# In three opening slots of an attention and gated-MLP kernel, VectorE's weight passes move behind the second maxima, and GpSimd's q/k split behind its weight split

## The chip, the core and the metric

The kernel runs on one core of a Trainium2 chip. A core has TensorE (PE, matrix products and transposes), VectorE (DVE), ScalarE (ACT), GpSimd (POOL) and SyncE (SP), which here only issues transfers. Each engine works through its own list of instructions in order and waits on semaphores for the others. The metric is the device time of one execution in microseconds, 771.0 us as the median of three runs of the kernel before.

## The reference

For 8 batches with 8 heads, 576 positions and 64 values per head:

```python
scores = (1.0 / np.sqrt(D)) * np.matmul(q, k.transpose(0, 1, 3, 2))
scores = np.where(block_i >= block_j, scores, -1000000000.0)   # blocks of 64 positions
attn = np.exp(scores - np.max(scores, axis=-1, keepdims=True))
attn = attn / (np.sum(attn, axis=-1, keepdims=True) + 1e-09)
x = np.matmul(attn, v)                      # then (8, 576, 512)
...
h = gelu_tanh(x @ w_in)                     # w_in 512 x 1024
u, v = h[..., :512], h[..., 512:]
v_n = (v - mu) / np.sqrt(var + 1e-06) * g_ln
v_s = np.einsum('ts,bsd->btd', w_sg, v_n) + b_sg[None, :, None]
out = x + (u * v_s) @ w_out
```

Everything is float32. Some of the weights arrive as 64-bit words (float64).

## The kernel before

The work is cut into 32 slots, one for a pair of heads (8 batches of 4 pairs). In a slot the kernel finishes the attention of pair n and begins the scores of pair n+1. To keep float32 accuracy on fast products, an operand is split into a high part (`qh`, `kh`, `wi_h`, `xh`) and the remainder (`ql`, `kl`, `wi_l`, `xl`), and three products high-high, low-high, high-low are summed.

For one pair (two heads, a = 0, 1), rows come in five groups i = 0 to 4 of growing width. `Scores.products` (L327) lets PE write scores to PSUM (`s`). `Scores.maximum` (L349) is DVE's: it copies the scores with the mask to `prob` and leaves the negated row maximum in `negm`. `Scores.exponent` (L364) is ACT's exponential of `prob` with that `negm`. The groups 4, 1 and 0 form the list `FIRST` (L388): eight maxima of up to 288 columns, here called the first maxima. `Scores.second` (L394) does groups 3 and 2: products, then four maxima of 448, 448, 320 and 320 columns (the second maxima), then four exponentials. `Values.turn` (L415) transposes `prob` on PE into `pA`, `pB`, `pC` and copies these to SBUF (`ptA`, `ptB`, `ptC`, half of them by DVE); `pB` and `pC` need the second exponentials. `Values.products` and `normalise` (L458, L477) multiply with v and scale (`ob`, `x`), and `split` (L485) makes `xh` and `xl`. `split_qk` (L112) splits the q and k of the pair after next on GpSimd: `qh`, `ql`, `kh`, `kl`, each for 576 columns; the next slot's scores read them.

While the first four slots run, the 64-bit weights are also converted. `load_weight` (L212) yields three times per group of parts (a part is 128 x 256): after the load and an ACTIVATE of ScalarE, after `Double.single` (L201), which on DVE is one TENSOR_SCALAR and two SCALAR_TENSOR_TENSOR for each part (the "passes over the weights", tile `w`), and after `split_weight` (L184), on GpSimd a CAST to `wi_h` and a subtraction to `wi_l`. Each call of `weight_half` runs one such third. The groups of the first four slots have 3, 2, 2 and 1 parts.

These four slots are written by `opening_slot` (L721). In them a switch (`written`) holds DVE, ACT and GpSimd to the order in which the code is written (PE always is); SP's transfers are placed by the scheduler. From the fifth slot on only PE's order is fixed, a scheduler places the rest, and the feed-forward products of a finished batch fill PE between the attention steps. The first of these are at the end of the fourth slot (`v_part`, tiles `accv`), which needs the converted weights of the v half.

Of the kernel before, what the change touches and what calls it, by code (L numbers as in the profile page):

```python
# [20 lines left out]
def kernel(  # L21
# [70 lines left out]
    def copy(e, dst, src):  # L92
        f = {"v": vector.tensor_copy, "a": scalar.copy, "g": gpsimd.tensor_copy}[e]
        return f(dst, src)
# [9 lines left out]
    def load_qk(n):  # L104
        b, h = PAIRS[n]
        q_f = sp.tile([P, S], F32, tag="q_f", name="q_f", bufs=1)
        k_f = sp.tile([P, S], F32, tag="k_f", name="k_f", bufs=1)
        nc.sync.dma_start(q_f, qT[b, h : h + 2].rearrange("a d s -> (a d) s"))
        nc.sync.dma_start(k_f, kT[b, h : h + 2].rearrange("a d s -> (a d) s"))
        raw[n] = (q_f, k_f)  # L110

    def split_qk(n):  # L112
        out = []
        for x, t in zip(raw.pop(n), "qk"):
            hi = sp.tile([P, S], F32R, tag=t + "h", name=t + "h", bufs=1)
            lo = sp.tile([P, S], F32R, tag=t + "l", name=t + "l", bufs=1)
            if n == 0:
                copy("v" if t == "q" else "a", hi, x)
                vector.tensor_tensor(lo, x, hi.bitcast(F32), op=ALU.subtract)
            else:  # L120
                copy("g", hi, x)
                behind["G"] = gpsimd.tensor_tensor(lo, x, hi.bitcast(F32), op=ALU.subtract)
            out += [hi, lo]
        qk[n] = out

    def load_v(n):
        b, h = PAIRS[n]
        v_f = v_bufs[n % 2]
        cols = slice(h * D, (h + 2) * D)
        nc.sync.dma_start(  # L130
            v_f[:, : NT - 1, :],
            v[b, : (NT - 1) * P, cols].rearrange("(j p) d -> p j d", p=P),
        )
        nc.sync.dma_start(v_f[:TAIL, NT - 1, :], v[b, S - TAIL :, cols])
        vals[n] = v_f
# [156 lines left out]
    def weight_half():  # L292

        while weights:
            said = next(weights[0][1], None)
            if said is not None:
                return said
            weights.popleft()
# [416 lines left out]
    def split_pending():  # L715

        for f in pending:
            f()
        pending.clear()

    def opening_slot(n, va):  # L721

        va.turn(0, "A")
        va.turn(1, "A")
        va.turn(0, "B")
        va.turn(1, "B")
        va.inverse()
        split_pending()
        va.turn(0, "C")
        va.turn(1, "C")  # L730
        load_v(n + 1)
        load_qk(n + 2)
        nx = Scores(n + 1)
        for p in nx.FIRST:
            nx.products(*p)
        va.turn_sums()
        weight_half()
        for p in nx.FIRST:
            nx.softmax(*p)
        weight_half()  # L740
        if n < Q - 1:
            nx.second()
            split_qk(n + 2)
            weight_half()
            va.products()
            va.normalise()
            pending.append(va.split)
        else:
            weight_half()
            va.products()  # L750
            va.normalise()
            va.split()
            nx.second()
        nv = Values(n + 1, nx)
        if n == Q - 1:
            nv.inverse()
            split_qk(n + 2)
        return nx, nv
# [118 lines left out]
```

## Time and profile before

| what | before |
|---|---|
| median of the runs shown | 771.0 us (768.85, 771.0, 771.5) |
| the profiled execution | 770.48 us, its span 768.7 us |
| busy share of the span | PE 98%, DVE 63%, ACT 57%, POOL 39% |
| first maximum of pairs 1, 2, 3, 4 | 15.68, 31.70, 45.79, 59.73 us |

The span runs from the first to the last instruction; the execution's own time is 1.8 us longer. A row of the timeline gives start, duration, engine, the line of the code (L60 for nearly all, a helper that records every operation), the operation, `out<-in` with sizes, and in brackets the idle time ahead of it with the engine that ended it. PEld is PE's loading of its stationary operand, which overlaps with the products. A busy share over the whole span hides that the opening slots have other limits than the rest, so the prediction looks at these by themselves.

### The profile page before, as it was taken

To read this page: it belongs to the slowest core of one execution; us is meant where nothing else is said; L and a number is where in the kernel's file an instruction comes from. 1 tells how busy PE (TensorE), PEld (TensorE's weight loads), DVE (VectorE), ACT (ScalarE), POOL (GpSimd) and SP (SyncE) were. 2 spreads that over 40 slices of the span, in tenths; PEclk is the share of its full clock that TensorE was granted. 3 is DMA by queue.
4 is the path that set the end of the run, shared out by engine and by line. 5 is a ranking of instruction groups with operands and counts; after the bars stand their busy time and mean duration, and the time that the engine had idled before them with its cause. 6 is when DMAs were issued, how large, how long until landed. Compare 5 with 4: busy or idle time off the path is not lost.

```text
span 768.7 us, 18262 instructions
## 1 busy us (share of the span) xinstructions
PE 751.7 (98%) x7106; PEld 711.2 (93%) x7106; DVE 483.5 (63%) x1477; ACT 438.3 (57%) x1096; POOL 299.2 (39%) x382
## 2 busy tenths in 40 slices
PE   8779998999999999999999999999999999999998
PEld 8778997989999899999999899998999989998998
DVE  6898789775945468544776348663495644942632
ACT  6666868558734767337754377544874467731600
POOL 3666695544234333243434234341234522322121
PEclk9989999999999999999999999999999999999999
DMA  8235233224232213312242112511124211120032
GB/s 261 82 103 178 64 107 92 77 90 133 85 119 62 63 64 109 94 47 63 64 140 78 33 61 76 172 48 48 49 91 141 63 42 53 53 88 17 1 124 93
DMA packets 46922, 65.84 MB, mean 86 GB/s; under 512 B 4082, under 2 KB 22514, under 8 KB 46836
## 3 DMA queue, kind: packets, MB, share of 16 engines
q1 hardware_dynamic: 46836, 64.67, 27.0%
q8 instruction: 56, 0.92, 0.5%
q14 instruction: 30, 0.25, 0.1%
HBM read 45.78 MB, written 18.87 MB: 84 GB/s over the span
## 4 chain that ended last, share of the span: by engine, by line
PE 92%; DVE 6%; ACT 1%; issue 1%; DMA 0%; POOL 0%; SPq 0%; DVEq 0%; ACTq 0%; POOLq 0%
PE accs L60 15%; PE accv L60 14%; PE acco L60 13%; PE accu L60 12%; PE s L60 10%; PE ob L60 10%; PE pB L60 5%; PE pC L60 5%; PE pA L60 3%; PE pd L60 2%; DVE w L60 2%; DVE prob L60 2%; PE pe L60 1%; ACT prob L60 1%; DVE vv L566 1%
## 5 line engine op out<-in xcount | busy, mean ns | idle before, releaser
L60 ACT ACTIVATE prob<-prob,negm 128x576 f32<-128x576 f32 (+3 forms) x320 | 176.4, 553 | 72.2 <-DVE negm L60 69.4
L60 DVE CUSTOM_DVE_ANT_0 prob<-s,mask 128x288 f32<-128x288 f32 (+3 forms) x320 | 121.5, 424 | 47.7 <-PE s L60 47.0
L60 POOL TENSOR_TENSOR xh<-x,xh 128x64 fp32r<-128x64 f32 x32 | 10.4, 325 | 205.5 <-DVE xh L60 145.4
L60 POOL TENSOR_TENSOR gl<-u,gh 128x288 fp32r<-128x288 f32 x64 | 51.8, 813 | 95.7 <-DVE gh L60 95.5
L60 PE MATMUL accu<-xh,wi_h 128*128 128x288 f32 x256 | 78.4, 306 | 0.0
L60 PE MATMUL accs<-ws_h,vh 128*128 128x288 f32 x256 | 77.9, 304 | 0.0
L60 PE MATMUL acco<-gh,wo_h 128*128 128x288 f32 x256 | 77.6, 303 | 0.0
L60 PE MATMUL accs<-ws_h,vl 128*128 128x288 f32 x256 | 75.6, 295 | 1.3 <-DVE vl L60 1.3
L60 PE MATMUL acco<-gl,wo_h 128*128 128x288 f32 x256 | 75.5, 295 | 0.0
L60 PE MATMUL accu<-xl,wi_h 128*128 128x288 f32 x256 | 75.5, 295 | 0.0
L60 PE MATMUL accs<-ws_l,vh 128*128 128x288 f32 x256 | 75.5, 295 | 0.0
L60 PE MATMUL accu<-xh,wi_l 128*128 128x288 f32 x256 | 75.4, 295 | 0.0
L60 PE MATMUL acco<-gh,wo_l 128*128 128x288 f32 x256 | 75.3, 294 | 0.0
L60 PE MATMUL accv<-wi_h,xh 128*128 128x512 f32 x160 | 65.3, 408 | 0.0
L60 DVE TENSOR_TENSOR u<-accs,u 128x288 f32<-128x288 f32 x64 | 29.1, 455 | 54.4 <-PE accs L60 53.9
L60 PE MATMUL accv<-wi_l,xh 128*128 128x512 f32 x160 | 63.0, 393 | 0.0
L60 PE MATMUL s<-kh,qh 64*128 64x288 f32 (+4 forms) x384 | 62.6, 322 | 0.0
L60 ACT ACTIVATION_READ_ACCUMULATOR prob<-prob,negm 128x1 f32 x320 | 59.9, 187 | 0.0
L60 PE MATMUL s<-kh,ql 64*128 64x288 f32 (+4 forms) x384 | 58.4, 301 | 0.0
L60 PE MATMUL s<-kl,qh 64*128 64x288 f32 (+4 forms) x384 | 57.3, 299 | 0.0
L60 ACT COPY vv<-accv 128x512 f32<-128x512 f32 x32 | 18.6, 581 | 67.1 <-PE accv L60 67.1
L60 PE MATMUL pB<-ident,prob 128*128 128x128 f32 x320 | 43.6, 283 | 8.5 <-DVE negm L60 6.8
(113 smaller groups left out, 2108.5 us busy)
## 6 DMA issues: line engine op xcount, KB each, us to landing
q_f<-in_qT SPq DMA_DIRECT2D x32, 288.0 KB, 3.6
k_f<-in_kT SPq DMA_DIRECT2D x32, 288.0 KB, 2.8
spill<-x SPq DMA_DIRECT2D x32, 288.0 KB, 2.9
xr<-spill SPq DMA_DIRECT2D x32, 288.0 KB, 2.9
out_T<-xr SPq DMA_DIRECT2D x32, 288.0 KB, 2.1
v_f<-in_v SPq DMA_DIRECT2D x32, 256.0 KB, 3.2
w<-in_w_in SPq DMA_DIRECT2D x16, 256.0 KB, 4.8
xr<-in_w_out SPq DMA_DIRECT2D x8, 256.0 KB, 2.7
```

What stands on the lines that cost most here:

```text
L60: return lambda *a, **k: pin(method(*a, **k), self.letter)
L566: tc.keep_in_program_order(nc.vector.scalar_tensor_tensor(x, x, stats[:rows, st, 0:1], g_bc[:rows, :], op0=ALU.subtract, op1=ALU.mult))
```

## The change

In the first three slots (n = 0, 1, 2) the second scores, maxima and exponentials are written ahead of DVE's passes over the weights, and GpSimd's weight split ahead of `split_qk`. The fourth slot keeps its order.

```diff
         weight_half()
         for p in nx.FIRST:
             nx.softmax(*p)
-        weight_half()
         if n < Q - 1:
             nx.second()
+            weight_half()
+            weight_half()
             split_qk(n + 2)
-            weight_half()
             va.products()
             va.normalise()
             pending.append(va.split)
         else:
+            weight_half()
             weight_half()
             va.products()
             va.normalise()
```

On DVE, in the second slot (the first maxima, of groups 4, 1 and 0, end above these rows; `prob0_3` is head 0, group 3; the ISA rows of `negm` alone read out the maximum that the row before them found). A piece of the difference:

```order
 L60 ISA prob1_0_115,negm_523<-s_539,mask_94 64x64
 L60 ISA negm_523 64x1
+L60 ISA prob0_3_111,negm_522<-s_586,mask_94 128x448
+L60 ISA negm_522 128x1
+L60 ISA prob1_3_121,negm_523<-s_587,mask_94 128x448
+L60 ISA negm_523 128x1
+L60 ISA prob0_2_109,negm_522<-s_598,mask_94 128x320
+L60 ISA negm_522 128x1
+L60 ISA prob1_2_119,negm_523<-s_599,mask_94 128x320
+L60 ISA negm_523 128x1
 L60 TENSOR_SCALAR w_566<-w_349 128x256
 L60 SCALAR_TENSOR_TENSOR w_566<-w_349,w_566 128x256
```

The four second maxima, which stood behind the slot's last pass over `w` and just ahead of `x`, now follow the first maxima at once.

On GpSimd, in the same slot (`q_f`, `k_f` are the loaded q and k; `w_566` and `w_570` the slot's two weight parts):

```order
-L60 CAST qh_616<-q_f_516 128x576
-L60 TENSOR_TENSOR ql_617<-q_f_516,qh_616 128x576
-L60 CAST kh_620<-k_f_517 128x576
-L60 TENSOR_TENSOR kl_621<-k_f_517,kh_620 128x576
 L60 CAST wi_h_125<-w_566 128x256
 L60 TENSOR_TENSOR wi_l_126<-w_566,wi_h_125 128x256
 L60 CAST wi_h_125<-w_570 128x256
 L60 TENSOR_TENSOR wi_l_126<-w_570,wi_h_125 128x256
+L60 CAST qh_620<-q_f_516 128x576
+L60 TENSOR_TENSOR ql_621<-q_f_516,qh_620 128x576
+L60 CAST kh_624<-k_f_517 128x576
+L60 TENSOR_TENSOR kl_625<-k_f_517,kh_624 128x576
```

The four instructions of the q/k split moved behind the four of the weight split; the buffers' numbers differ because they are now made later.

On SP the load of the next q, which waits for GpSimd to be done with the present one, moved behind the next v load and the store of `x` (`spill`), here in the first slot:

```order
+L130 DMA v_f0_101<-in_v 128x4x128
+L483 DMA spill_456<-x_453 128x576
 L108 DMA q_f_516<-in_qT 128x576
-L130 DMA v_f0_101<-in_v 128x4x128
-L483 DMA spill_456<-x_453 128x576
 L109 DMA k_f_517<-in_kT 128x576
```

The k load keeps its place. PE's and ScalarE's instructions stand in the same order as before.

## The prediction

> **What bounds the kernel now.** I read the busy shares and the chain of waits first, then the stretch that the change touches.
>
> ```profile
> PE 751.7 (98%) x7106; PEld 711.2 (93%) x7106; DVE 483.5 (63%) x1477; ACT 438.3 (57%) x1096; POOL 299.2 (39%) x382
> PE 92%; DVE 6%; ACT 1%; issue 1%; DMA 0%; POOL 0%; SPq 0%; DVEq 0%; ACTq 0%; POOLq 0%
> ```
>
> TensorE (PE) carries the chain nearly everywhere; VectorE (DVE) holds 6% of it. Part of those 6% lies in the three opening slots, where no feed-forward products exist yet. I measure a slot from the first maximum of one pair (`prob<-s,mask 128x288`) to the first maximum of the next: from 15.68, 31.70 and 45.79 us, the last ending at 59.73. The windows view gives their lengths and busy times (columns: length, then PE, PEld, DVE, ACT and POOL (GpSimd), granted clock, DMA):
>
> ```profile
> 15.68:31.70 16.02, 12.02 (x135) 10.63 (x135) 13.92 (x41) 10.01 (x30) 9.84 (x13) 0.89 0.47 142
> 31.70:45.79 14.09, 11.96 (x135) 10.86 (x135) 12.66 (x39) 9.28 (x28) 8.20 (x10) 0.88 0.29 92
> 45.79:59.73 13.94, 11.82 (x135) 10.72 (x135) 12.66 (x38) 9.17 (x28) 8.24 (x12) 0.88 0.34 98
> 59.73:100.00 40.27, 40.27 (x405) 36.45 (x405) 33.02 (x106) 31.52 (x83) 27.47 (x41) 1.00 0.37 117
> ```
>
> In the slots PE idles 2 to 4 us each while DVE is busy for nine tenths. From 59.73 on PE has no idle time, so whatever moves that instant moves the end by as much. I therefore price one number: the sum of three slot lengths, 44.05 us. Waits within them:
>
> ```profile
> PE pB L60 <- DVE negm L60: 6.8, 3, 3.5
> DVE prob L60 <- PE s L60: 2.6, 3, 1.2
> DVE ptB L60 <- PE pB L60: 0.6, 2, 0.4
> ```
>
> PE waits 6.8 us for the second maxima; DVE itself waits only 3.2 us for PE. So DVE's own row of work sets the slot. Here it is in the third slot, with the undisturbed weight part of the fourth slot (62.22) and the last part of the first slot (23.40) under it:
>
> ```profile
> 45.79 0.46 DVE L60 CUSTOM_DVE_ANT_0 prob<-s,mask 128x288 f32<-128x288 f32 x1 [0.88 <-PE s L60]
> 48.27 0.28 DVE L60 TENSOR_SCALAR w<-w 128x256 uint32<-128x256 uint32 x1
> 49.73 1.51 DVE L60 TENSOR_SCALAR w<-w 128x256 uint32<-128x256 uint32 x1
> 51.28 2.31 DVE L60 SCALAR_TENSOR_TENSOR w<-w 128x256 uint32<-128x256 uint32 x2
> 53.51 0.61 DVE L60 CUSTOM_DVE_ANT_0 prob<-s,mask 128x448 f32<-128x448 f32 x1
> 55.42 0.68 DVE L60 TENSOR_TENSOR x<-ob,rb 128x512 f32<-128x512 f32 x1
> 59.73 0.46 DVE L60 CUSTOM_DVE_ANT_0 prob<-s,mask 128x288 f32<-128x288 f32 x1 [0.60 <-PE s L60]
> ...
> 62.22 0.28 DVE L60 TENSOR_SCALAR w<-w 128x256 uint32<-128x256 uint32 x1
> 62.54 0.95 DVE L60 SCALAR_TENSOR_TENSOR w<-w 128x256 uint32<-128x256 uint32 x2
> ...
> 23.40 0.48 DVE L60 TENSOR_SCALAR w<-w 128x256 uint32<-128x256 uint32 x1
> 25.27 0.61 DVE L60 CUSTOM_DVE_ANT_0 prob<-s,mask 128x448 f32<-128x448 f32 x1
> ```
>
> A weight part is one TENSOR_SCALAR and two SCALAR_TENSOR_TENSOR. Alone it takes 1.27 us (62.22 to 63.49). In the third slot two parts take 5.24 us (48.27 to 53.51), because GpSimd splits q and k at that moment: the same TENSOR_SCALAR needs 0.28 us at 48.27 and 1.51 us at 49.73, ending just after GpSimd's 1.48-us subtraction. The two engines take turns.
>
> ```profile
> 48.69 0.84 POOL L60 CAST qh<-q_f 128x576 fp32r<-128x576 f32 x1 [2.57 <-PE s L60]
> 49.61 1.48 POOL L60 TENSOR_TENSOR ql<-q_f,qh 128x576 fp32r<-128x576 f32 x1
> 51.84 1.46 POOL L60 TENSOR_TENSOR kl<-k_f,kh 128x576 fp32r<-128x576 f32 x1
> ...
> 40.51 0.40 POOL L60 CAST wi_h<-w 128x256 fp32r<-128x256 f32 x1
> 40.99 0.73 POOL L60 TENSOR_TENSOR wi_l<-w,wi_h 128x256 fp32r<-128x256 f32 x1
> ...
> 67.19 0.66 POOL L60 CAST qh<-q_f 128x576 fp32r<-128x576 f32 x1
> 67.93 1.44 POOL L60 TENSOR_TENSOR ql<-q_f,qh 128x576 fp32r<-128x576 f32 x1
> 69.31 0.74 POOL L60 CAST kh<-k_f 128x576 fp32r<-128x576 f32 x1
> ```
>
> **The change, part by part.** Instructions stay the same in kind and number; PE's and ScalarE's orders are untouched, and so is everything from the fourth slot on.
>
> (1) The second maxima no longer stand behind the weight parts. ScalarE's second exponentials can follow its first ones, so PE's 6.8 us of waiting for `negm` goes. On DVE alone this only reorders work. (2) GpSimd's q/k split no longer runs beside the weight parts, so these lose most of the turn-taking. Both gain for DVE. (3) The price: GpSimd now splits q and k *behind* the weights, whose split waits for DVE's last part. The next slot's first scores read that qh, kh and kl. Before, the split ended at 53.30 (51.84 + 1.46), 6.4 us ahead of the next first maximum, and cost the path nothing; that cover is now gone. So the stall moves from "PE waits for negm" to "PE waits for kl", and the new slot is a sum along DVE, GpSimd and PE:
>
> a. eight first maxima: 45.79 to 48.27, 2.48.
> b. four second maxima: 53.51 to 55.42, 1.91.
> c. the first weight part, GpSimd still: 1.27, less some 0.07 by which such rows overlap, 1.2.
> d. the second part while GpSimd splits the first. Never seen alone; between 1.27 (no turn-taking) and 1.87 (23.40 to 25.27, the one part that ran beside a weight split). There its TENSOR_SCALAR waited too (0.48 against 0.28); now GpSimd can only start after it, so I take 1.87 - 0.20 = 1.67.
> e. GpSimd's split of that last part: 0.40 and 0.73 with their gap, 40.51 to 41.72, plus 0.07 of release: 1.28.
> f. the q/k split: undisturbed 4.3 (67.19 to the end of kh at 70.05, where kl could start, plus 1.44), in the old place 4.61 (48.69 to 53.30). DVE's cast of xh now meets it once, at about the price that CAST qh shows, 0.84 - 0.66 = 0.18. I take 4.5.
> g. from kl to the first maximum: PE's remaining products and the release, 0.70, from this row to 45.79, 0.64, plus 0.06:
>
> ```profile
> 45.15 0.29 PE L60 MATMUL s<-kl,qh 64*128 64x288 f32 x2
> 47.78 0.36 PE L60 MATMUL s<-kl,qh 64*128 64x448 f32 x2
> 56.95 1.85 PE L60 MATMUL pC<-ident,prob 128*128 128x128 f32 x10
> 13.48 1.25 PE L60 MATMUL pC<-ident,prob 128*128 128x128 f32 x10
> ```
>
> Sum 13.74, against 14.09 and 13.94: -0.35 and -0.20. The first slot has three parts, 13.74 + 1.67 = 15.41 against 16.02: -0.61. Together **-1.2 us**. With d and f at their low ends the loops are 13.14 and 14.41, together -3.4; with c, d and f at their high ends 14.12 and 15.99, together +0.2.
>
> What runs beside it costs nothing: DVE's x, ptA, ptB, xh and ptC take at most 3.7 us after d (from 55.42 to 59.13, where the wait of 0.60 before 59.73 begins; a wait for pB is in it), while e and f take 5.8. The q load now goes out after the spill and when the later ql is done, about 11 us into a slot; the next CAST qh stands 8.5 us into the following one, 11 us later, and the load takes 3.6. GpSimd's xh and xl follow kl, run beside DVE's maxima (0.61 us at 53.51, though GpSimd was at its weight split from 53.30 on) and are done before the next weight part.
>
> ```profile
> q_f<-in_qT SPq DMA_DIRECT2D x32, 288.0 KB, 3.6
> ```
>
> **The clock is the second term.** A windows view cut into stretches of 3.41 us shows the granted clock (the column after the POOL entry):
>
> ```profile
> 20.61:24.02 3.41, 1.80 (x28) 1.50 (x24) 2.82 (x5) 1.29 (x6) 3.25 (x5) 1.00 0.59 169
> 37.67:41.09 3.42, 1.29 (x11) 0.87 (x9) 3.32 (x9) 1.01 (x3) 3.18 (x6) 1.00 0.51 164
> 41.09:44.50 3.41, 3.41 (x18) 3.41 (x18) 3.15 (x10) 2.86 (x9) 0.74 (x2) 0.50 0.42 130
> 51.33:54.74 3.41, 1.53 (x15) 1.03 (x11) 3.31 (x7) 0.97 (x5) 3.25 (x5) 1.00 0.46 106
> 54.74:58.15 3.41, 3.17 (x15) 3.18 (x16) 3.00 (x11) 2.88 (x10) 0.97 (x2) 0.50 0.48 167
> ```
>
> After a stretch with PE busy 1.29 or 1.53 us the clock is halved for one stretch; after 1.80 it isn't. Today the half clock falls on the transposes (pC takes 1.85 instead of 1.25) and costs what DVE waits for PE: the 3.2 us above. These are inside the old slot lengths and leave with them. In the new slot the second exponentials end at 2.41 us (54.16 to 56.57) after the first ones, which are over at 51.72 (54.16 less the wait of 2.44), 5.93 us into the slot:
>
> ```profile
> 54.16 0.67 ACT L60 ACTIVATE prob<-prob,negm 128x448 f32<-128x448 f32 x1 [2.44 <-DVE negm L60]
> 56.57 0.56 ACT L60 COPY ptA<-pA 128x512 f32<-128x512 f32 x1
> ```
>
> So pC ends about 8.9 us in; then PE idles until kh (8.54 + 2.9 = 11.4) and, after 0.5 us of products, until kl (13.0). Some 3.6 idle us of 4.1 stand together, and the halved stretch now falls behind them, on the scores. PE's last product for the first of the second maxima ends at 48.14, 2.35 us into the slot, and DVE wants it at 2.48: only 0.13 us of slack. A halved stretch costs PE up to 1.7 us (half of 3.41), a lucky one falls on later products and costs 0. The middle, 0.85, in two of the three slots, is **+1.7 us**; bounds 0 and 5.1.
>
> [...]
>
> **Sum.** -1.2 + 1.7 = +0.5 us on the profiled execution, which took 770.48 with a span of 768.7. That gives 771.0, which is also the median of the runs shown (768.85 to 771.5). Forecast: no change that can be told; a measurement of this kernel tells about 0.3%, 2.3 us.
>
> **Rivals.**
> *The clock stays full* (chance 0.22). The gap is cut by the scores that need only kh, and 1.80 busy us kept the clock up. Then -1.2 stands alone: 769.3, and 767.1 at the low ends of d and f. About a third of this case is below the 0.3% bound.
> *GpSimd doesn't gate* (0.03). If the q/k split were hidden, DVE's row would bound: 2.48 + 1.91 + 1.2 + 1.67 + 3.34 (x to ptC without the wait) + 0.95 for the scores = 11.6, 2.4 less per slot: -7, 763.5. Against it: the split would have to end by 10.6, but starts at 8.5 and takes at least 4.3.
> *Slower: the half clock lands on the scores in every slot* (0.15). Then DVE's second maxima, now with 0.13 us of cover instead of 5.2 us of weight parts, wait 1.7 each time: -1.2 + 5.1 = +3.9, 774.4; 775.8 with the high ends. It decides from 3.5 us of clock loss on, two full hits.
> That the order isn't changed as said is ruled out by the rows of the new order.
>
> **Chances.** Forecast 0.60, the three rivals 0.22, 0.03 and 0.15. Faster: 0.08 + 0.03 + 0.01 = 0.12; slower 0.15; same 0.73. The range 768.8 to 773.3 takes in the open clock with middle prices and one full hit more than forecast, and leaves out the outer ends of the rivals, 2 in 10.
>
> **What would show it.** Right: DVE's slots of about 15.4, 13.7 and 13.7 plus clock losses; weight parts after the second maxima in 2.9 us a pair instead of 5.2; "PE pB waits for negm" gone and "PE s waits for POOL kh or kl" in its place, 2 to 4 us a slot; POOL in the chain where DVE's w stood; the 0.50 stretches just after a kl. Wrong: slots near 11.6 (GpSimd hidden), weight parts still at 2.6 us each (turn-taking stays), or a first maximum that doesn't follow kl by 0.7 us.

## The result, and the profile after

| what | before | after |
|---|---|---|
| median of five executions each | 770.13 us (768.66 to 771.5) | 775.68 us (773.3 to 776.41) |
| ratio, with its 95% interval | | 1.0069 [1.0045, 1.0092] |
| the profiled execution | 770.48 us, span 768.7 | 773.3 us, span 771.5 |
| first maximum of pairs 1, 2, 3, 4 | 15.68, 31.70, 45.79, 59.73 us | 15.47, 31.32, 47.04, 62.57 us |
| sum of the three slots | 44.05 us | 47.10 us |

The kernel became 0.7% slower, about 5.5 us. The page's busy shares and its chain of waits, of the kernel after:

```profile
PE 752.5 (98%) x7106; PEld 711.2 (92%) x7106; DVE 480.2 (62%) x1477; ACT 437.9 (57%) x1096; POOL 298.8 (39%) x382
PE 89%; DVE 3%; POOL 2%; ACT 2%; DMA 2%; issue 1%; SPq 0%; POOLq 0%; ACTq 0%
```

GpSimd (POOL) is in the chain now, and DVE's share fell from 6% to 3%. In the slots the chain reaches DVE's last weight pass over ScalarE's exponentials (ACT, 2%) and not over DVE's maxima. That this link costs time isn't shown: the part's two SCALAR_TENSOR_TENSOR take 1.38 us here (39.11) and 1.38 us in the second slot of a kernel below, the second half of the change alone (33.17), whose chain has no such link there. DVE is busy 3.3 us less (480.2 against 483.5). The slots, and with them the fourth, in the windows view of the kernel after (length, then PE, PEld, DVE, ACT and POOL busy, granted clock, DMA):

```profile
15.47:31.32 15.85, 11.01 (x133) 9.67 (x133) 12.71 (x41) 9.81 (x30) 9.02 (x12) 0.95 0.39 124
31.32:47.04 15.72, 12.63 (x133) 11.23 (x133) 11.34 (x39) 9.06 (x28) 7.85 (x12) 0.83 0.28 90
47.04:62.57 15.53, 13.21 (x135) 11.82 (x135) 11.56 (x38) 9.22 (x28) 8.07 (x12) 0.79 0.25 78
62.57:81.48 18.91, 18.91 (x178) 16.51 (x178) 15.45 (x48) 12.84 (x36) 12.97 (x21) 1.00 0.59 176
```

DVE has 1.1 to 1.3 us less to do in each slot (11.34 against 12.66 in the second), yet the second and third slots are 1.6 us longer, at a granted clock of 0.83 and 0.79 where before it was 0.88. The fourth slot is as long as before (18.91 us, there 59.73 to 78.64). The waits of these slots in the kernel after (in all, times, longest):

```profile
POOL wi_h L60 <- DVE w L60: 22.8, 7, 7.4
DVE prob L60 <- PE s L60: 10.5, 6, 2.7
PE s L60 <- POOL kh L60: 7.2, 3, 3.8
PE s L60 <- POOL kl L60: 2.9, 3, 1.1
```

PE's wait for `negm` is gone. PE now waits 10.1 us for kh and kl, 3.4 a slot, and DVE waits 10.5 us for PE. GpSimd idles some 7 us at the start of each slot, until the first weight part is done, and is the one waited for at its end. The second slot on DVE, after:

```profile
31.32 0.46 DVE L60 CUSTOM_DVE_ANT_0 prob<-s,mask 128x288 f32<-128x288 f32 x1 [2.69 <-PE s L60]
...
33.81 0.07 DVE L60 DVE_READ_ACCUMULATOR2_ANT negm<- 64x1 f32 x1
35.68 0.62 DVE L60 CUSTOM_DVE_ANT_0 prob<-s,mask 128x448 f32<-128x448 f32 x1 [1.80 <-PE s L60]
...
37.60 0.29 DVE L60 TENSOR_SCALAR w<-w 128x256 uint32<-128x256 uint32 x1
...
38.79 0.29 DVE L60 TENSOR_SCALAR w<-w 128x256 uint32<-128x256 uint32 x1
...
40.41 0.68 DVE L60 TENSOR_TENSOR x<-ob,rb 128x512 f32<-128x512 f32 x1
...
42.66 1.51 DVE L60 CAST xh<-x 128x576 fp32r<-128x576 f32 x1
47.04 0.46 DVE L60 CUSTOM_DVE_ANT_0 prob<-s,mask 128x288 f32<-128x288 f32 x1 [2.27 <-PE s L60]
```

The two weight parts take 2.81 us (37.60 to 40.41), where they took 5.24. But ahead of the second maxima, at 35.68, DVE stands idle for 1.80 us. PE shows why. Its timeline has the first scores for the second slot above, then a piece of that slot's second scores, and at the foot the first scores for the third slot:

```profile
28.61 0.40 PE L60 MATMUL s<-kh,qh 64*128 64x288 f32 x2 [3.81 <-POOL kh L60]
30.10 0.61 PE L60 MATMUL s<-kl,qh 64*128 64x288 f32 x2 [0.95 <-POOL kl L60]
...
35.07 0.57 PE L60 MATMUL s<-kl,qh 64*128 64x448 f32 x2
...
44.75 0.40 PE L60 MATMUL s<-kh,qh 64*128 64x288 f32 x2 [2.14 <-POOL kh L60]
46.23 0.40 PE L60 MATMUL s<-kl,qh 64*128 64x288 f32 x2 [0.95 <-POOL kl L60]
```

The last product for the first of the second maxima ends at 35.64 (35.07 + 0.57), 4.3 us into the slot; before it was 2.35. Between 30.10 and 35.64 PE waits for nobody, but these two products take 0.57 us where the same two took 0.36 before (47.78). The windows of 3.41 us show the reason, the granted clock (after POOL):

```profile
26.25:29.67 3.42, 0.53 (x4) 0.30 (x4) 2.35 (x5) 1.21 (x2) 3.27 (x3) 1.00 0.39 114
29.67:33.08 3.41, 2.98 (x23) 2.92 (x24) 1.76 (x9) 0.00 (x0) 2.06 (x4) 0.50 0.60 189
33.08:36.49 3.41, 3.41 (x20) 2.61 (x20) 1.61 (x11) 2.60 (x9) 0.00 (x0) 0.50 0.01 2
43.32:46.73 3.41, 1.03 (x12) 0.80 (x14) 1.45 (x2) 0.72 (x2) 3.33 (x5) 1.00 0.30 87
46.73:50.15 3.42, 3.42 (x25) 3.02 (x25) 2.56 (x16) 0.54 (x2) 1.14 (x2) 0.50 0.27 86
50.15:53.56 3.41, 3.41 (x26) 2.94 (x28) 2.16 (x9) 3.41 (x12) 0.00 (x0) 0.50 0.00 0
```

After a stretch in which PE is busy 0.53 or 1.03 us, the clock is halved for two stretches, 6.83 us, not for one. They begin among the first scores and cover the second scores too. Such a run of halved stretches is called a closing below.

### The profile page after: what moved, and what is told of

The parts are those of the page before. It is cut to its first block, busy times and chain, and to the rows that moved or that the text cites. A ratio compares the mean times of both kernels' runs of the same rounds, so it can differ in the third digit from the quotient of the medians.

```text
span 771.5 us, 18262 instructions
## 1 busy us (share of the span) xinstructions
PE 752.5 (98%) x7106; PEld 711.2 (92%) x7106; DVE 480.2 (62%) x1477; ACT 437.9 (57%) x1096; POOL 298.8 (39%) x382
## 4 chain that ended last, share of the span: by engine, by line
PE 89%; DVE 3%; POOL 2%; ACT 2%; DMA 2%; issue 1%; SPq 0%; POOLq 0%; ACTq 0%
PE accs L60 15%; PE accv L60 14%; PE acco L60 13%; PE accu L60 12%; PE s L60 10%; PE ob L60 10%; PE pC L60 4%; PE pB L60 4%; PE pA L60 3%; PE pd L60 2%; ACT prob L60 2%; PE pe L60 1%; DMA k_f<-in_kT 1%; POOL kl L60 1%; DVE vv L566 1%
## 5 line engine op out<-in xcount | busy, mean ns | idle before, releaser
L60 POOL TENSOR_TENSOR xh<-x,xh 128x64 fp32r<-128x64 f32 x32 | 10.5, 328 | 197.0 <-DVE xh L60 136.9
L60 PE MATMUL s<-kl,qh 64*128 64x288 f32 (+4 forms) x384 | 59.4, 309 | 3.0 <-POOL kl L60 2.9
L60 PEld LDWEIGHTS s<-kh,qh 64*128 64x128 f32 x384 | 37.4, 191 | 17.5 <-POOL kh L60 7.9
```

What stands on the lines that cost most here:

```text
L60: return lambda *a, **k: pin(method(*a, **k), self.letter)
```

## The experiments

My theory after the result: the sum of the steps without the clock holds (15.41 + 13.74 + 13.74 = 42.89 us for the three slots), and the rest, 47.10 - 42.89 = 4.2 us, is the clock, halved because PE idles while GpSimd splits q and k. The first rival: the sum itself is too small, and the wait for GpSimd costs what the clock seems to. The second: one of the two halves of the change does the harm. The kernel before was run beside each; its median was 770.44 us in both groups of timed runs.

**Keep PE busy in the gap.** The kernel after with 20 transposes of the identity, whose result nobody reads, in the gap after `pC`. They take 0.12 us each at full clock (20 in 2.40 us, at 25.32 below).

```diff
         nx = Scores(n + 1)
+        if n:
+            warm(bank("warm"), 20)
         for p in nx.FIRST:
             nx.products(*p)
```

> The changed kernel, and in slots 2 to 4 twenty more transposes of the identity on PE, into a PSUM bank that nobody reads, between the transposes of pC and the next scores, where PE idles 3.8, 2.1 and 1.3 us for GpSimd's kh. Nothing else moves. Theory (clock): the idle stretch halves the granted clock, and the half clock falls on the scores that DVE's second maxima wait for. With the gap filled the 0.50 stretches before 65 us are gone, the slots shrink from 15.85, 15.72, 15.53 to about 15.4, 13.7, 13.7, and the time falls by 4 us or more from 775.7, to 769 to 771.5. Rival (GpSimd alone): what costs is PE's wait for the q/k split itself; then the fill changes nothing, slots stay near 15.7 and the time at 775 to 776.

Measured: 770.77 us (12 executions), ratio to before 1.0002 [0.9989, 1.0015]. The slots in the windows view, and the two ends of the filled gap on PE:

```profile
15.77:31.17 15.40, 12.93 (x153) 11.35 (x153) 12.74 (x42) 9.79 (x30) 8.57 (x12) 1.00 0.39 127
31.17:46.41 15.24, 13.91 (x155) 12.72 (x155) 11.36 (x38) 9.07 (x28) 8.28 (x12) 0.89 0.31 96
46.41:60.19 13.78, 12.51 (x155) 11.37 (x155) 11.26 (x38) 9.07 (x28) 8.28 (x12) 1.00 0.29 87
```

```profile
25.32 2.40 PE L60 MATMUL warm<-ident 128*128 128x128 f32 x20 [0.24 <-DVE x L60]
28.94 0.40 PE L60 MATMUL s<-kh,qh 64*128 64x288 f32 x2 [1.21 <-POOL kh L60]
```

The two slots at full clock last 15.40 and 13.78 us; the prediction's sums for them are 15.41 and 13.74. So the sum stands, and the first rival falls: PE's first scores still stand until GpSimd's kh and kl are there, 13.2 us into the slot (28.94 - 15.77) against 13.1 in the kernel after, and the 5.5 us are gone. The second slot, with one half-speed stretch left (31.03 to 34.44), is 1.5 us longer than the sum: here one stretch cost that much.

**Fewer transposes.** The same with 8 instead of 20.

```diff
+            warm(bank("warm"), 8)
```

> As warm_gap, but with eight transposes instead of twenty in each of the three gaps, 0.9 us of PE's idle 3.8 to 1.3. Theory (clock): the loss goes with the time at half clock, so this stands between the changed kernel and warm_gap, 771 to 775.5, with a mean granted clock between 0.987 and 0.997 and some closings of one stretch instead of two. Rival (the fill helps for another reason, such as the PSUM bank it takes, which shifts the banks after it): the bank is taken here too, so the time is warm_gap's, 770 to 771.

Measured: 773.49 us (770.21 to 776.3, 12 executions), ratio 1.0038 [1.0016, 1.006], between the kernel after and the filled one. Its single executions are the clearest sign: those at a mean granted clock of 0.997 took 770.21, 770.29 and 770.4 us, those at 0.986 took 775.52, 776.29 and 776.3. One and the same program, and 6 us with the clock. In the profiled one (774.56 us) two of its three closings lasted one stretch instead of two. The rival, that only the PSUM bank of the transposes matters, would have given 770 to 771 and falls.

**The kernel after again**, beside these.

> The changed kernel once more, beside the others on one chip. Both theories: 773 to 776.5, slots of 15.5 to 16 us, two or three pairs of halved stretches before 66 us.

Measured: 776.49 us (775.46 to 777.3, 6 executions), ratio 1.0074 [1.0058, 1.0091]. Its profiled execution took 776.63 us and shows what the first profile (the fastest of five, 773.3 us at a clock of 0.990, the others at 0.987 to 0.988) did not: a third closing. The windows view, third and fourth slot:

```profile
47.15:63.29 16.14, 12.74 (x133) 11.48 (x133) 11.34 (x39) 9.08 (x28) 8.25 (x12) 0.82 0.26 76
63.29:84.74 21.45, 21.45 (x178) 18.88 (x178) 15.44 (x47) 12.83 (x36) 12.46 (x21) 0.88 0.48 153
```

Cut into stretches of 3.41 us:

```profile
58.38:61.79 3.41, 0.53 (x4) 0.30 (x4) 2.22 (x3) 1.21 (x2) 3.33 (x3) 1.00 0.38 110
61.79:65.20 3.41, 3.14 (x24) 3.08 (x25) 1.91 (x13) 0.00 (x0) 1.98 (x6) 0.50 0.64 172
65.20:68.61 3.41, 3.41 (x31) 3.08 (x31) 1.70 (x9) 2.75 (x10) 1.01 (x2) 0.50 0.46 162
```

PE is halved across the start of the fourth slot, which has no idle time on PE: 21.45 us instead of 18.91. In all the clock costs 47.50 (15.84, 15.52 and 16.14) - 42.89 in the three slots and 2.54 in the fourth, 7.2 us here against 4.2 in the first profile.

**The first half of the change alone**: the second maxima ahead of the passes, and `split_qk` where it was, ahead of the weight split on GpSimd.

```diff
-        weight_half()
         if n < Q - 1:
             nx.second()
+            weight_half()
             split_qk(n + 2)
             weight_half()
...
         else:
             weight_half()
+            weight_half()
```

The second call under `else` keeps the fourth slot as it was.

> One half of the change: the second maxima stand ahead of DVE's weight passes, but GpSimd splits q and k ahead of the weights, as before. Theory (the late q/k split does the harm): kl is ready 7.5 us into a slot, so PE's scores wait for nothing of GpSimd's, PE's idle time stays short, no halved stretch falls before 60 us or one at most; DVE's row bounds, 2.48 + 1.91 + two passes beside the q/k split (at most 5.24) + 3.34 = at most 13.0 a slot, 14.8 in the first. That is 3 us less than before, up to 6 if the passes meet only part of the q/k split: 764 to 767. Rival (the second maxima, put straight behind PE's second scores, do the harm, since they have no cover): slots of 14 and more, DVE waiting for PE s at the 448-wide maxima, 770 or more.

Measured: 765.02 us (762.39 to 766.59, 6 executions), ratio 0.9925 [0.9905, 0.9944]: faster. In the profiled execution (762.39 us, the fastest of the six) the clock stayed full; the windows view of its first and second slot:

```profile
15.07:28.96 13.89, 11.30 (x145) 9.95 (x143) 13.44 (x41) 9.35 (x30) 8.17 (x12) 1.00 0.50 150
28.96:40.69 11.73, 10.31 (x131) 9.32 (x131) 11.42 (x39) 9.06 (x29) 8.41 (x12) 1.00 0.42 125
```

Its weight passes in the second slot, from the first row to the second:

```profile
33.34 0.28 DVE L60 TENSOR_SCALAR w<-w 128x256 uint32<-128x256 uint32 x1
...
37.53 0.68 DVE L60 TENSOR_TENSOR x<-ob,rb 128x512 f32<-128x512 f32 x1
```

DVE is busy 11.42 of 11.73 us: its row alone sets the slot, 2.4 us shorter than before. That is the length the prediction gave for "GpSimd doesn't gate" (11.6): GpSimd's split of q and k starts early, and only the weight split stands behind DVE. That the two lengths agree is in part luck: beside the q/k split the passes take 4.19 us (33.34 to 37.53), not the 2.87 of that sum, and the 0.95 it adds for the scores isn't waited for.

**The second half alone**: `split_qk` behind the weight split, the second maxima still behind the passes.

```diff
             nx.second()
-            split_qk(n + 2)
             weight_half()
+            split_qk(n + 2)
```

> The other half: DVE keeps its order (weight passes, then second maxima), GpSimd splits the weights ahead of the next q and k. Theory (the price of the change is that four maxima, 1.91 us, stand ahead of the passes for which GpSimd waits): the chain of the sum loses its term b, 2.48 + 1.2 + 1.67 + 1.28 + 4.5 + 0.70 = 11.8 a slot, 13.5 in the first; passes 2.9 us a pair; second maxima at 5.35 us, when ScalarE is just through with the first exponentials, so PE idles under 2 us and the clock stays full: 37.2 us for three slots instead of 44.0, 763 for the whole. Rival (any q/k split behind the weights makes PE wait and halves the clock): slots of 14 to 16 us, a halved stretch in each, 771 to 776.

Measured: 762.64 us (761.72 to 762.74, 4 executions), ratio 0.9894 [0.9876, 0.9912]: the fastest kernel here, 13.9 us ahead of the kernel with both halves (776.49 beside it). Second slot, in the windows view, and on DVE and GpSimd:

```profile
29.20:40.89 11.69, 10.46 (x135) 9.18 (x133) 11.38 (x40) 9.17 (x28) 8.11 (x12) 1.00 0.45 134
```

```profile
31.67 0.28 DVE L60 TENSOR_SCALAR w<-w 128x256 uint32<-128x256 uint32 x1
...
34.48 0.61 DVE L60 CUSTOM_DVE_ANT_0 prob<-s,mask 128x448 f32<-128x448 f32 x1
...
35.78 0.67 POOL L60 CAST qh<-q_f 128x576 fp32r<-128x576 f32 x1
...
38.64 1.41 POOL L60 TENSOR_TENSOR kl<-k_f,kh 128x576 fp32r<-128x576 f32 x1
40.89 0.44 DVE L60 CUSTOM_DVE_ANT_0 prob<-s,mask 128x288 f32<-128x288 f32 x1
```

It is the predicted sum less its term b: the second maxima (1.91 us) run while GpSimd splits weights, instead of ahead of the passes for which GpSimd waits. First maxima 2.47, two parts 2.81, to the q/k split 1.30, the split 4.27, to the next first maximum 0.84: 11.69 us, against 13.74 - 1.91 = 11.83. So neither half is the harm by itself; both together put 1.9 us of maxima on the path and leave PE without work for longer (0.53 and 1.03 us busy of 3.41 ahead of the two closings of the first profile; here the closing that is left came behind 2.18), and the clock closed for 6.83 us each time. The three slots sum to 37.00 us here (13.36, 11.69 and 11.95): of the 10.1 us to the 47.10 of the kernel with both, 5.9 are the path (42.89 - 37.00) and 4.2 the clock. The expectation that the clock stays full missed once: it was halved for one stretch from 41.41, in the third slot, where weight passes stand ahead of the second maxima, and that slot is only 0.26 us longer than the second.

**Does the kernel before lose to the clock as well?** The kernel before with 14 such transposes at the start of a slot, in its gap ahead of `pA`.

```diff
     def opening_slot(n, va):
+        if n:
+            warm(bank("warm"), 14)
         va.turn(0, "A")
```

> The kernel before, and in slots 2 to 4 fourteen transposes of the identity on PE into a PSUM bank that nobody reads, ahead of the transposes of pA, where PE has time to spare (after them it waits 1.7 us or more for the second maxima). Theory (the halved stretches cost the kernel before what DVE waits for PE, 3.2 us): most of them go, the second and third slot fall from 14.1 and 13.9 to about 13.6, and the time by 1 to 2 us from 770.4, to 768.4 to 769.4, at a granted clock of 0.996 or more. Rival (before, the half clock falls on work that has time to spare): 770 to 771 whatever the clock does.

Measured: 768.87 us (767.65 to 771.32, 12 executions), ratio 0.9988 [0.9971, 1.0005], not told apart from no change. Seven of the executions took 767.65 to 769.22 us at a mean granted clock of 0.995 to 0.998, the other five 770.61 to 771.32 at 0.992 or 0.993. The windows view, second and third slot and a later one:

```profile
31.51:44.31 12.80, 12.13 (x155) 10.94 (x153) 12.49 (x38) 8.70 (x28) 7.31 (x12) 1.00 0.32 90
44.31:57.28 12.97, 11.87 (x150) 10.69 (x149) 12.66 (x39) 9.16 (x29) 8.49 (x12) 1.00 0.28 90
113.29:137.16 23.87, 19.97 (x171) 18.94 (x169) 18.94 (x48) 16.58 (x37) 12.14 (x14) 0.86 0.25 74
```

The second slot is 1.29 us shorter than before (14.09), and the fourth begins 2.5 us earlier (57.28 against 59.73). In this profiled execution, the slowest of the twelve (771.32 us), the first slot still has its closing, and the clock closed once more, at 122.74, for 6.83 us: that slot takes 23.87 us, before 20.23 (116.07 to 136.30), and the gain is given back. The two slots also say what the change is worth without the clock: at full clock the old order takes 12.80 and 12.97 us, the new one 13.74 by its sum and 13.78 in the filled kernel. The new order is the longer one, by some 0.8 to 0.9 us a slot.

**Why two stretches?** The kernel after, with 6 or 10 transposes behind the first half of the first scores, so that they run in the halved stretch itself.

```diff
-        for p in nx.FIRST:
+        for j, p in enumerate(nx.FIRST):
             nx.products(*p)
+            if n and j == 0:
+                warm(bank("warm"), 6)
```

> The changed kernel with six 128x128 transposes of the identity, whose result nobody reads, behind the first half of each next pair's first scores, so that they run inside the halved stretch and not ahead of it. It is about how long the clock stays at half, not about the time. Theory A (the stretch goes on for a second 3.41 us while PE does mostly the scores, which use 64 of its 128 rows, and ends when transposes over all 128 rows fill a part of it, as they do in the kernel before): in the changed kernel five closings of five lasted 6.83 us; here at least two of three last 3.41. Theory B (the length is settled by what went ahead of the closing, an idle PE): nothing changes ahead of it, so the closings still last 6.83 us. In both the transposes cost the first maxima 0.7 to 1.4 us a slot; by B about 778 us, by A, with up to 1.8 us less waiting for the second maxima where a stretch is short, 774 to 777.

> The same with ten transposes (1.2 us at full clock, 2.4 at half). Theory A: all closings last one stretch of 3.41 us, more surely than with six. Theory B: 6.83 us as in the changed kernel. Time by A 775 to 778 us, by B about 780.

Measured, in one execution each: 779.22 and 779.59 us, the kernel before 768.62 beside them. In the slots the closings lasted 6.83 and 10.24 us with six, and 6.83, 3.41 and 3.41 with ten. The longest of them, with six, and a short one, with ten, in the windows views:

```profile
46.45:49.86 3.41, 2.63 (x16) 2.13 (x16) 1.40 (x8) 0.00 (x0) 2.40 (x4) 0.50 0.43 145
49.86:53.28 3.42, 3.42 (x22) 3.03 (x23) 1.24 (x8) 0.54 (x2) 0.00 (x0) 0.50 0.00 0
53.28:56.69 3.41, 3.41 (x26) 2.96 (x28) 2.17 (x9) 3.41 (x12) 0.00 (x0) 0.50 0.00 0
```

```profile
47.34:50.76 3.42, 3.42 (x22) 2.94 (x22) 1.40 (x8) 0.00 (x0) 1.11 (x2) 0.50 0.29 86
```

Theory A foresaw at least two short ones of three with six transposes and three with ten; there were none and two. Theory B foresaw 6.83 us each time and has neither the 3.41 nor the 10.24. What decides the length stays open: the stretches from 49.86 and 47.34 read almost alike, and only the first goes on at half.

## Why the prediction was wrong

**What bounds the kernel** was right. The slots set the instant from which PE has no idle time, and the span grew by what they grew by: 3.05 us, less 0.21 for the earlier start at 15.47, is 2.84; the spans differ by 2.8. But the view behind "From 59.73 on PE has no idle time" ends at 100 us. In the kernel before PE is busy only 17.07 of the 20.23 us from 116.07 to 136.30, and there the kernel before with its gaps filled lost what it had gained by 57.28. So an earlier fourth slot need not reach the end.

**The change part by part, (1) to (3)**, was right: the wait for `negm` is gone, the parts take 2.81 us a pair (said: 2.9), and the stall went to kh and kl (3.4 us a slot; said: 2 to 4).

**Terms a to g** were right. In the second slot, from the rows above: b is 1.92 (35.68 to 37.60; said 1.91), c 1.19 (1.2), d 1.62 (1.67). On GpSimd, in the same slot:

```profile
41.72 0.66 POOL L60 CAST qh<-q_f 128x576 fp32r<-128x576 f32 x1
...
44.77 1.40 POOL L60 TENSOR_TENSOR kl<-k_f,kh 128x576 fp32r<-128x576 f32 x1
```

So e is 1.31 (40.41 to 41.72; said 1.28), f 4.45 (41.72 to 46.17; said 4.5) and g 0.87 (46.17 to 47.04; said 0.70). Their sum is shown by the filled gap, 15.40 and 13.78 against 15.41 and 13.74. What f adds for DVE's cast of xh was priced for GpSimd alone. DVE pays more: the cast takes 1.51 us beside `ql`, where it took 0.40 in the second slot before (43.91). That costs nothing, since DVE still has 2.27 us to spare before 47.04.

**The clock term failed**, "the middle, 0.85, in two of the three slots, is +1.7 us". It measured 4.2 us in the first profile (0.44, 1.98 and 1.79 by slots) and 7.2 in the other. Three things in it were wrong:

- "the clock is halved for one stretch": in all five closings of the two profiles of the kernel after it was two. The bound of 1.7 us for one hit came from one stretch; DVE's waits ahead of the second maxima were 1.80 and 1.81 us, the whole price and more.
- "a lucky one falls on later products and costs 0", so the middle was taken. Nothing in the rows spoke for luck: PE's gap ends at kl, the scores follow at once, and the cover was 0.13 us. A stretch that begins near kl falls on the scores, as those from 29.67 and 46.73 did (kl's first products at 30.10 and 46.23). The full price was the one to take.
- Only three slots were counted. The kernel after can also be halved where its third gap ends, at the start of the fourth slot, and there it cost 2.54 us.

So the rival "the half clock lands on the scores in every slot" came true in its mechanism and its size: it said 774.4 to 775.8, deciding from 3.5 us of clock loss on, and the median is 775.68. It came a little otherwise than told: the closings are longer, two in the first profile and three in the other, and the last of those three costs the fourth slot. A chance of 0.15 was too little for it, and the range ended at 773.3, with one full hit more than the forecast.

That the old clock losses "leave with" the old slots was right in the sum, since the filled gap reaches the sum of the new terms. But it made the comparison look mild. The -1.2 us sets new slots at full clock against old ones with their losses; at full clock on both sides the second and third slot grow by 0.8 to 0.9 us each, as the filled kernel before showed. And losses come back, in a place where DVE has no weight passes left to hide them.

The clock closed behind PE's gap of 3.81 us (28.61) and behind the one of 2.14 us (44.75) alike.

## What to carry to other kernels

Before a wait of TensorE is moved, look at what runs right behind it: here the halved clock fell on what followed the gap, for 6.83 us behind gaps of 3.81 and 2.14 us in the kernel after. A closing cost 1.0 to 1.3 us a slot where it fell on the old order's transposes (13.94 against 12.97, 14.09 against 12.80), 1.5 us or more where it fell on products that DVE waited for, and about 0.26 us where weight passes covered it. Price a closing of the clock at its full length, two stretches of 3.41 us in all five closings of the kernel after, unless a row shows cover for it. And when two reorderings meet on one path, cost each alone as well: here each gains (0.75% and 1.06%), and together they lose 0.7%, because the one moves work ahead of the very step for which the other makes PE wait, and behind the longer wait the clock closed.

## What was not expected of the hardware

The halved clock came here for one, two or three times 3.41 us: 3.41 in the kernel before (41.09 to 44.50), 6.83 in the kernel after (29.67 to 36.49) and 10.24 with six transposes (46.45 to 56.69). How many stretches followed is not told by PE's busy share ahead of the closing: after 1.03 us of 3.41 busy there were two in the kernel after (43.32 above), and in the kernel before, after as much, one:

```profile
24.03:27.44 3.41, 1.03 (x7) 0.72 (x7) 3.31 (x11) 1.51 (x5) 2.90 (x5) 1.00 0.02 6
```

Nor does a share tell whether it closed: the fastest kernel, the second half alone, was halved from 41.41 for one stretch behind this one, more than half busy, while before it stayed full after 1.80 us (20.61).

```profile
38.00:41.41 3.41, 2.18 (x28) 1.68 (x25) 3.38 (x8) 1.79 (x4) 2.94 (x4) 1.00 0.69 192
```

One program differed by 6 us between its executions, the one with 8 transposes, together with its mean granted clock (770.21 us at 0.997, 776.3 at 0.986).
